# One core's attention and Mish MLP on Trainium2: the same steps in a newly annealed order

## The chip, the cores and the metric

The kernel runs on one core of a Trainium2 chip. Its five engines run side by side, each through its own instructions in order: TensorE (PE, matrix products), VectorE (DVE), ScalarE (ACT), GpSimd (POOL) and SyncE (SP, which only issues DMAs here). They meet at semaphores. The metric is the device time of one launch in microseconds, as the median of repeated runs.

## The reference, cut to what matters

```python
def _attn_ref(q, k, v):            # 8 batches, 8 heads, 576 rows, head size 64
    q_s = exp(q - max(q, axis=-1));  q_s /= sum(q_s, axis=-1) + 1e-09
    k_s = exp(k - max(k, axis=2));   k_s /= sum(k_s, axis=2) + 1e-09
    kv = einsum('bhsd,bhse->bhde', k_s, v)
    return einsum('bhsd,bhde->bhse', q_s, kv)

def _moe_ref(x, w_in, w_out):      # x 4608 x 512, w_in 512 x 2048, w_out 2048 x 512
    h = x @ w_in
    g = h * tanh(where(h > 20, h, log1p(exp(min(h, 20)))))
    return g @ w_out
```

The heads of the attention's result are laid side by side as the rows `x` of the MLP.

## The kernel before

The kernel is a set of small steps (functions such as `a_ktt`, `h_part`, `w_fetch`) and one long string, `ORDER` (line 23), of 2551 tokens. A loop at the end (line 971) takes the tokens one by one and calls the step that each names (dictionary `stages`, line 947) with its numbers; letters behind the numbers name the PSUM banks (a to h) that the step opens, or the engine (v, p, s) that it uses. Every step issues its instructions to its engines as it is called, and `manual_schedule` keeps that order. So `ORDER` is the order of every engine's queue, of the DMAs on SP's and POOL's queues too, and nothing else in the kernel decides when something runs, other than the waits that follow from data and buffers. Some tokens name the same step on another engine: `RL`, `RM` and `RS` make the low half of a weight on GpSimd, ScalarE or VectorE; `RO` and `RD` a weight's low part on GpSimd or VectorE; `GA` and `G` a copy on ScalarE or VectorE.

The products are made of high and low halves: each 32-bit factor is split into two parts in the multiplier's own format, and three of the four part products are summed in PSUM (the three matmuls of `h_part`, `out_part`, `first_product`, `second_product`). The weights come as 64-bit numbers and are put together in integer steps.

The stages, in the order in which PE goes through them:

- **The opening.** SP loads K transposed (`LK`), Q (`LQ`), V (`V`) and weights (`R`). K: `MK` (DVE, column maximum), `KA` (ACT, subtract), `KT` (PE, transposes), `EK` (ACT, exponential). Q: `MQ` (DVE), `SQ` (POOL), `EQ` (ACT), `Q` and `QZ` (DVE), `QM` (POOL), `T` (PE, transposes), `TC` (ACT, copy out of PSUM). Then `KP` (PE, K times V), `S` (DVE, scaled into `kvt`), `XP` and `XT` (PE, Q times it, the main rows and the tail rows), `Z` and `ZL` (ACT and DVE, the high and low part of `x`), `ZT` (ACT, the tail). A weight goes through `RA` (ACT), `RL`/`RM`/`RS`, `RB` and `RC` (DVE), `RH` (ACT, the high part), `RO`/`RD` (the low part). `FI` n (`idle`, line 403) runs n multiplications of 128 columns, two instructions each, whose result nobody reads. `EX` is one small exponential on ACT.
- **Three batches in the plain way.** `H` and `HM` (PE, `x` times `w_in`; token `H` 4f+t is the t-th quarter of the f-th column block), `Y` (ACT, Mish), `GA`/`G` and `GL` (high and low part), `O` and `OP` (PE, times `w_out`). Beside it the attention of the other batches goes on in pairs (`PX`, `PK` on PE; `QM`, `SQ` on POOL; `T` from 8 on by DVE), and the weights are mixed for the rest (`WW`, `WM`, `WH`, `WL`) and written to a DRAM buffer `ws` (`WK`, `WP`, DMAs on SP).
- **The other five batches, and the tail rows of all eight as a sixth, in three pairs (k = 0, 1, 2)**, by seven products of half-size blocks in place of eight. `A` k.n.p (PE, the first product, six matmuls) goes into the banks px, pz and py, and `C`, `J`, `N` take it out (ACT copy, DVE sum, ACT Mish). `GX`, `GH`, `GK` mix and split the result, `BB` k.f.p (PE, the second product) multiplies it with `w_out` blocks, `DP`, `DJ` and `DS` take the result out and store it. `BM`, `DK` and `DT` are the same for the last product, in halves. The weights for `A` and `BB` come back from `ws` through six slots: `F` e (`w_fetch`, line 813, a DMA of 512 KB on POOL's queue) may start when the last product that uses slot e - 6 is done, and the products of slot e wait for its landing.

Of the kernel before, what the change touches and what calls it, by code (L numbers as in the profile page):

```python
# [33 lines left out]
Y6 RC14 RL19 GA6 H28f GL5 R25 O4 RS18 RA16g GL6 RA15h RH14 RB16 RA18e RO14 RB15 RH17 RC16 RM30 H29 RC15 RO17 RM21 H30
RB18 RA19h R26 H31 R31 RH16 QM4 RB19 RM20 H32g RC19 Y7 H33 RO16 RM24 RC18 H34 RA21h G7 H35 RB21 O5 QZ5 Y8 RC21 RH15
QM5 GL7 RA20h G8 RA23e RO15 RH18 RB20 O6 RH19 RB23 RO18 WK1 GL8 RC23 RD19 RA24e RH21 H40g RB24 R27 WK0 H41 RC24 H42
RC20 RH24 H43 RH23 RO24 T4ef Y10 H36h TC4 LQ6 RO21 G10 R28 H37 RA22f RS22 L6 H38 RL31 GL10 V6 H39 RB22 O7 Y9 RC22 RL26
GA9 RH22 GL9 RM25 MQ6 RH20 T5ef MK6 RM27 RO20 H44h RA25g LQ7 MK7 TC5 ST2 H45 RB25 RO23 WK2 RA27e H46 RA26f RB27 O8 SQ6
# [5 lines left out]
OP13.0 ZT6 Z6 H60g MQ8 ST6 Z7 U8.0 OP14.3 WH1.1 MS8 H61 ZL6 H62 ZT7 MT8 WH1.0 ZL7 SQ8 H63 U8.1 OP14.2 WL1.0 EQ8 HM16h
Q8 LQ9 ST7 WL1.1 LK10 Y15 WP1.0 G15 WP1.1 HM17e GL15 Y16 RH31 V8 GA16 RO31 QW8 HM18f Y17 MK10 GL16 WM2.0p MQ9 OP15.1
Y18 QV8 OP14.0 MS9 WM2.1p OP15.2 OP15.0 WH2.0 KB10 QM8 OP15.3 EV0.0v EV0.1s WH2.1 HM19g G17 GA18 T8 KM10 WL2.0 MT9
GL17 WP2.0 SQ9 HM20h EV0.2v UE10.0 WK15 GL18 EV0.3s EQ9 PK6eb LQ10 OP16.0 S8 OP16.3 WL2.1 OP17.0 Q9 WP2.1 HM23f QW9
V10 MQ10 ES0.0 QV9 MS10 WW3v OP16.2 OP17.3 QM9 Y19 OP16.1 GA19 WM3.0p OP17.1 Y20 GL19 OP17.2 U10.0 WM3.1p HM21e T9
UE10.1 WH3.0 MT10 SQ10 GA20 OP18.3 WW4v EQ10 OP19.3 WH3.1 OP18.2 WL3.0 Q10 OP18.0 WP3.0 Y21 WL3.1 HM22g LQ11 GA21
U10.1 QW10 GL20 LK12 WP3.1 GL21 OP18.1 Y22 WM4.0p OP19.2 Y23 G22 PX8he QV10 GL22 QM10 OP19.0 Z8 OP20.2 Z9 ZL8 OP19.1  # L50
ZL9 OP20.1 G23 WM4.1p OP20.3 MQ11 PK8eh GL23 WH4.1 WW5v MS11 HM24g ZT8 MT11 WH4.0 T10 ST8 SQ11 S10 ES0.1 WL4.1 OP21.3
WL4.0 WP4.1 OP22.3 EQ11 ZT9 OP21.1 Q11 LQ12 WP4.0 OP23.3 QW11 HM25e WK13 QV11 MK12 QM11 KB12 WK14 OP20.0 KM12 T11
OP21.0 UE12.1 OP21.2 UE12.0 WM5.0p WK12 HM26h U12.0 WM5.1p MQ12 Y24 Y25 ST9 OP22.1 V12 Y26 OP23.1 WH5.1 MS12 WL5.1
# [983 lines left out]
```

## Time and profile before

| | us |
|---|---|
| median of three runs (791.91, 792.03, 793.3) | 792.03 |
| the profiled execution, its own time | 792.54 |
| its span, first to last instruction | 790.8 |
| chain that ended last: share of PE | 93% of the span |
| weight fetches `ws<-ws`, issue to landing (median of 172) | 4.5 |

A group's row in the profile gives the line, the engine, the operation, what it writes and reads, its shape, how many there are, the busy time and the mean of one. In a row of a timeline the first two numbers are the start and the length in microseconds, and the bracket at the end is the engine's idle time before it, with what ended it. Matmuls overlap: a stream of 512-column matmuls on PE starts one every 0.227 us (twelve in 2.72), though one alone is shown with some 0.39.

### The profile page before, as it was taken

What the parts mean: (1) busy time and instruction counts of PE and PEld (TensorE: products, weight loads), DVE (VectorE), ACT (ScalarE), POOL (GpSimd) and SP (SyncE); (2) the same over time, 40 slices, a digit from 0 to 9 for tenths busy, and PEclk for the clock granted to TensorE, in tenths of its full rate; (3) what the DMA queues carried; (4) which work ended last, traced back from release to release, by engine and by line L of the source; (5) the groups of instructions that cost most, each with busy time, mean ns of one, the idle gap of its engine ahead of it and who ended that gap; (6) DMA issues with size and microseconds to landing.
All of it is one profiled execution on the core that took longest, in us unless ns stands there. A gap on an engine that the chain in (4) does not pass through costs nothing.

```text
span 790.8 us, 12668 instructions
## 1 busy us (share of the span) xinstructions
PE 782.1 (99%) x4640; PEld 632.4 (80%) x4640; DVE 535.7 (68%) x874; ACT 496.5 (63%) x945; POOL 274.8 (35%) x350
## 2 busy tenths in 40 slices
...
GB/s 349 375 347 235 344 155 212 169 240 166 211 258 133 180 62 216 319 256 237 290 237 235 246 254 235 161 244 143 276 193 208 231 222 212 207 165 236 168 232 188
DMA packets 76685, 178.86 MB, mean 226 GB/s; under 512 B 15568, under 2 KB 28112, under 8 KB 76624
## 3 DMA queue, kind: packets, MB, share of 16 engines
q0 software_dynamic: 24768, 90.19, 36.3%
q1 hardware_dynamic: 51712, 87.74, 33.1%
...
q14 instruction: 25, 0.20, 0.1%
q10 hardware_dynamic: 144, 0.13, 0.0%
...
## 4 chain that ended last, share of the span: by engine, by line
PE 93%; DMA 2%; DVE 2%; ACT 1%; issue 1%; SPq 0%; POOL 0%; DVEq 0%; POOLq 0%; ACTq 0%
PE px L833 16%; PE ph L646 16%; PE po L684 15%; PE qx L850 12%; PE qz L850 8%; PE py L833 8%; PE qy L850 8%; PE pz L833 4%; PE px L533 2%; PE pt L568 2%; DMA ws<-ws 1%; DMA q<-in_q_dram 1%; PE pt L533 0%; PE pq L510 0%; DMA ws<-wi 0%
## 5 line engine op out<-in xcount | busy, mean ns | idle before, releaser
L816 POOL DMA_DIRECT2D ws<-ws x172 | 92.6, 540 | 337.1 <-PE qx L850 78.4
L833 PE MATMUL px<-xh,ws 128*128 128x512 f32 x384 | 129.0, 392 | 0.9 <-DMA ws<-ws 0.9
L883 ACT CAST gs<-g 128x1024 fp32r<-128x1024 f32 x84 | 87.2, 1052 | 66.2 <-PE qx L850 28.9
L219 DVE TENSOR_TENSOR gs<-g,gs 128x1024 fp32r<-128x1024 f32 x84 | 101.8, 1230 | 31.5 <-ACT gs L883 31.3
L684 PE MATMUL po<-wo,gh 128*128 128x512 f32 x384 | 119.9, 393 | 0.0
L850 PE MATMUL qx<-gs,ws 128*128 128x512 f32 x432 | 101.1, 389 | 0.0
L850 PEld LDWEIGHTS qx<-gs,ws 128*128 128x128 f32 x432 | 81.0, 188 | 17.6 <-issue 0.8
L646 PE MATMUL ph<-xs,wi 128*128 128x512 f32 x384 | 92.9, 392 | 1.1 <-DVE gl L219 0.7
L833 PEld LDWEIGHTS px<-xh,ws 128*128 128x128 f32 x384 | 72.1, 188 | 19.6 <-issue 2.5
L684 PEld LDWEIGHTS po<-wo,gh 128*128 128x128 f32 x384 | 71.1, 188 | 18.3 <-issue 3.2
L646 PEld LDWEIGHTS ph<-xs,wi 128*128 128x128 f32 x384 | 71.3, 188 | 17.7 <-DVE wc_in L271 1.3
L861 ACT COPY g<-px 128x512 f32<-128x512 f32 x72 | 41.1, 587 | 68.1 <-PE px L833 65.8
L865 DVE TENSOR_TENSOR g<-py,g 128x512 f32<-128x512 f32 x48 | 32.7, 684 | 63.7 <-PE py L833 38.8
L684 PE MATMUL po<-wo,gl 128*128 128x512 f32 x192 | 74.8, 390 | 0.0
L833 PE MATMUL px<-xl,ws 128*128 128x512 f32 x192 | 74.7, 389 | 0.0
L850 PE MATMUL qz<-gs,ws 128*128 128x512 f32 x288 | 67.7, 389 | 0.0
L850 PE MATMUL qy<-gs,ws 128*128 128x512 f32 x288 | 67.4, 389 | 0.0
L833 PE MATMUL py<-xh,ws 128*128 128x512 f32 x192 | 66.6, 390 | 0.0
L850 PEld LDWEIGHTS qy<-gs,ws 128*128 128x128 f32 x288 | 54.1, 188 | 11.2
L850 PEld LDWEIGHTS qz<-gs,ws 128*128 128x128 f32 x288 | 54.0, 188 | 11.2
L219 DVE TENSOR_TENSOR g<-g,g 128x1024 f32<-128x1024 f32 x48 | 57.7, 1217 | 1.9 <-ACT g L869 1.6
L491 POOL TENSOR_TENSOR qe<-qe,qs 128x576 f32<-128x576 f32 x24 | 29.6, 1231 | 74.2 <-DVE qs L487 45.3
(167 smaller groups left out, 1377.9 us busy)
## 6 DMA issues: line engine op xcount, KB each, us to landing
ws<-ws POOLq DMA_DIRECT2D x172, 512.0 KB, 4.5
...
```

What stands on the lines that cost most here:

```text
L219: eng.tensor_tensor(out, a, b, ALU.subtract)
L491: eng.tensor_tensor(q2, q2, z.unsqueeze(2).to_broadcast(list(q2.shape)), ALU.mult)
L533: nc.tensor.matmul((px, pt)[x][h][o], kvt[a, j], at[e + j]["qT"][x][a], start=True, stop=True)
L568: nc.tensor.matmul(pkv[i][j * D:(j + 1) * D], k, v_two[a, j, c], start=c == 0, stop=c == NR - 1)
L646: nc.tensor.matmul(gs[n], wi[f][:, a, t], x[:, z], start=t == 0 and i == 0, stop=t == HP - 1 and i == 2)
L684: nc.tensor.matmul(po[t], g[a][:, t * P:(t + 1) * P], wo[f][:, z], start=f == 0 and i == 0, stop=f == NF - 1 and i == 2)
L816: nc.gpsimd.dma_start(t.rearrange("p s z j c -> p s (z j c)"), ws[e % (NW // 2)].bitcast(F32R))
L833: nc.tensor.matmul(dst, w[:, a, j], xc[k, p][z][:, j].rearrange("p b s -> p (b s)"), start=p in (1, 2, 7) and j == 0 and i == 0, stop=j == ...
L850: nc.tensor.matmul(psb[key, k][m], w[:, a, m], g[:, z, f % 2], start=first and i == 0, stop=f == NH - 1 and i == 2, skip_group_check=p in ...
L861: nc.scalar.copy(g_quad(k, n)[q], psb[1, k, n])
L865: nc.vector.tensor_tensor(g, psb[2 if q == 0 else 7, k, n], g, ALU.add)
L883: nc.scalar.copy(t[:, 0], gq[k, h][G_PART[p]])
```

## The change

Only the string `ORDER` is replaced. The 2551 tokens are the same steps, but for 42 that do the same work on another engine, and the banks of some fifty are renamed; the counts of the `FI` tokens are 12, 3, 9, 4, 1, 1 before and 9, 1, 4, 12, 3, 1 after. 244 tokens keep their place; the others move 13 places on average, some writes of weights (`WK`) by up to 700. The last 70 tokens are the same. The new order is a new annealing run at a low temperature that starts from the order before, in a simulation whose DMA landings and instruction lengths are read from the trace of before. The parts at the opening, around `GL11`, around `F64` and around `F137`:

```diff
ORDER = """
-FI12a LK0 LQ0 LK1 LQ1 EX LQ2 LK2 LQ3 R0 LK3 MQ0 V0 V1 MK0 SQ0 MK1 R1 KA0 MQ1 KT0db EQ0 FI3a KA1 SQ1 Q0 EK0 KT1he V3
-MQ2 FI9a EK1 R2 QZ0 SQ2 MK2 EQ1 V2 Q1 KA2 QM0 EQ2 KT2hd R3 QZ1 RA0b MQ3 QM1 R4 T0ge EK2 Q2 FI4a RM0 R5 MK3 SQ3 TC0 R8
-KP0a QZ2 KA3 RB0 QM2 EQ3 T1fc R6 S0 KT3he TC1 Q3 RL1 R9 FI1d EK3 XP0gc RC0 RA1d QZ3 LK4 RH0 XT0ef RB1 QM3 T2ba Z0 R7
-KP2h RC1 ZT1 ZT0 Z1 RO0 ZL0 TC2 R10 FI1d ZL1 RM2 T3da PP S2 RA2b H0c RH1 RB2 H1 TC3 ST0 RO1 RS3 RA3g XP2ha RC2 RM4 R14
-RB3 RL5 H4b Z2 H5 Z3 R13 ZL2 RH2 XT2de ZL3 H2 RO2 ZT3 RC3 RA5h R11 H6 RA4f RB5 H7 ZT2 RL6 RH3 RB4 LQ4 RA6g H3 RC4 R15
-RA8d H8a RL8 RC5 H9 RD3 H10 RB6 Y0 RM7 H11 RB8 RL10 RH4 MK4 H12e RH5 RC6 H13 LK6 RA7f RO5 R12 RC8 Y1 H14 LK5 Y2 RB7
...
-RC25 RB26 WK5 RC26 RC27 H47 RD22 RH27 XT4ef RH26 H52g RO27 R29 ZT4 RH25 WK10 B6e H53 Y11 RL28 WW0v O9 MQ7 EQ6 WM0.0p
-WK9 KS6 ZT5 GA11 O10 WM0.1p WH0.0 Q6 RA29f WK7 RA28e QZ6 SQ7 WH0.1 RB28 RM29 RC28 EK6 H54 RO26 GL11 LK8 H55 RH28 RB29
-RO25 H48h WK11 EQ7 H49 Q7 RO28 H50 RC29 RW30 H51 RB30 H56e WL0.1 RH29 RC30 RW31 H57 WP0.1 WL0.0 H58 ST4 QZ7 H59 Y12
...
-XH1.4 A1.0.5 A1.1.2 N1.0.0 KB30 BB0.6.4 F66 C1.1.0 F63 C1.0.3 BB0.7.4 J1.0.3 QV28 A1.0.3 DJ0.2.0 QM28 DJ0.2.1 DS0.2.0
-A1.1.6 ST27 J1.1.0 F65 XL1.4 F64 A1.1.7 C1.1.2 T28 KM30 A1.2.2 F67 EQ29 A1.2.1 Q29 LQ30 A1.0.4 C1.2.0 F69 QW29 A1.1.5
...
-A2.3.4 F134 C2.5.0 A2.5.6 J2.3.2 F135 F138 J2.5.0 A2.7.1 GK2.1.1 N2.5.0 N2.4.2 N2.3.1 A2.5.7 A2.6.1 F137 A2.6.2 C2.6.0
-C2.5.2 A2.6.7 J2.6.0 F139 A2.5.5 A2.6.6 C2.5.3 J2.5.3 A2.5.3 C2.6.2 N2.5.3 N2.6.0 A2.6.5 F141 N2.4.3 F140 GH2.1.2
...
+FI9d LK0 FI1c FI4e LQ0 FI12d LQ1 LK1 LQ2 FI3c LK2 R0 MK0 LQ3 R1 MQ0 KA0 V1 KT0bh SQ0 EK0 LK3 MQ1 EQ0 SQ1 V2 MK1 V0 Q0
+KA1 R2 EQ1 MQ2 KT1af QZ0 EK1 SQ2 V3 MK2 RA0f Q1 R3 KA2 QM0 R6 RM0 QZ1 KT2dg MQ3 EQ2 QM1 R4 T0ch EX RB0 R5 TC0 MK3 SQ3
+T1ea EK2 Q2 TC1 KP0b RL1 QZ2 EQ3 LK4 RC0 R8 KA3 S0 RA1c QM2 KT3de RH0 Q3 XT0fh R7 EK3 XP0ag RB1 RO0 RM2 LQ4 QZ3 T2eb
+ZT1 RC1 Z0 KP2h QM3 ZT0 ZL0 RH1 R12 RA2f RO1 T3ad PP TC2 RB2 H0c R11 TC3 S2 H4b RM3 RC2 Z1 XP2ha R9 RA3e ZL1 RM4 RB3
+XT2df H1 R13 Z2 RL5 ZT3 FI1g LQ5 Z3 ZL2 H5 RH2 ZL3 H2 RA4g RO2 RC3 R10 H3 RB4 RH3 H6 RL8 RA5f RC4 H8a RB5 H9 MK4 RL6
+H10 Y0 RD3 LK6 RA6h H7 LK5 RC5 RA8g RL7 L4 H12e RB6 GA0 H13 RH5 R15 GL0 RA7f H11 RB8 RO5 R14 Y1 H14 RC6 ZT2 GA1 RB7
...
+R29 H52g WK1 RC27 RH26 H45 RD22 XT4ef WW0v H46 ZT4 ZT5 RM28 H53 WM0.0p RH27 MQ7 B6e H47 MK8 H48f RO26 Y11 H49 GA11 O9
+SQ7 GL11 KS6 EQ6 WM0.1p RA28h KB8 RB28 RO27 H50 EQ7 H51 WH0.0 RL30 KM8 Q7 O10 RH25 RC28 RA29e EK6 Q6 QZ6 RH28 H54 QZ7
...
+BB0.4.4 ZT26 XL1.5 BB0.5.4 J1.0.0 F61 F60 MT29 A1.0.6 F63 A1.1.1 C1.0.2 BB0.6.4 C1.1.0 ZT27 BB0.7.4 A1.1.6 DJ0.2.0 F65
+F64 QV28 A1.0.5 DJ0.2.1 A1.1.2 C1.0.3 J1.0.3 A1.0.3 J1.1.0 F66 QM28 A1.2.2 T28 N1.1.0 C1.1.2 XL1.4 A1.1.7 N1.0.1
+A1.1.5 F67 SQ29 A1.0.4 C1.1.3 A1.2.1 J1.0.2 EQ29 J1.1.3 LQ30 A1.1.3 Q29 C1.2.0 F69 V30 F68 J1.2.0 ST27 A1.3.1 DS0.1.1
...
+A2.6.1 C2.5.3 A2.5.7 A2.6.2 J2.5.3 F137 N2.5.3 A2.5.3 C2.6.0 F139 N2.0.2 J2.6.0 A2.6.6 N2.6.0 N2.4.1 A2.7.2 C2.6.2
```

More of the change, by code (lines that the diff above doesn't have):

```diff
@@ L34 @@
[L34 to L38, printed above, removed]
@@ L44 @@
[L44 to L48, printed above, removed]
@@ L49 @@
[L49 to L53, printed above, removed]
@@ new lines @@
+RA16g RL19 GA6 O4 RC17 RC14 RA15h RB16 RH17 R25 RH14 GL6 RO17 RC16 H28f RB15 RH16 RL20 H29 QZ4 RA18e H32g RC15 RS18
+H33 RA19h R26 RD14 RM21 H30 RB19 RO16 RH15 H31 RC19 H34 RL23 Y7 RB18 H35 GA7 RC18 RA21h O5 QZ5 RL24 Y8 RB21 RH18 GA8
+RC21 RO15 GL7 RA24h GL8 RA23e O6 QM4 RA20f RB24 RH19 RB20 RO18 RB23 MK6 H40g RO19 RC23 H41 RC24 R27 H42 RL22 RC20 RH24
+R28 H43 WK3 RS26 RH21 T4ef RD24 Y10 RL25 H36h MK7 TC4 H37 G10 RA22e LQ6 QM5 H38 GL10 ST0 H39 RB22 RA25g R30 O7 WK2 Y9
+RC22 RH20 GA9 RO20 RH23 GL9 RH22 RB25 RL27 RA26f T5he LK8 RD23 O8 TC5 LQ7 RB26 RA27e RO21 MQ6 RB27 SQ6 RC25 H44h RC26
@@ new lines @@
+MK14 OP24.3 Y26 OP23.2 WM5.1p G25 HM27f GL25 G26 WH5.1 GL26 WL5.1 OP24.0 WW6v Y27 OP24.1 GA27 OP25.0 GL27 PX10eg EQ12
+Q12 LQ13 PK10hf WP5.1 QW12 OP25.1 S12 V14 WH5.0 OP26.1 WK0 ZT10 Z10 WL5.0 OP24.2 KB14 QV12 OP25.3 KM14 MQ13 QM12
+UE14.0 OP26.3 ES0.2 Z11 HM28h WP5.0 U14.0 WM6.0p MS13 UE14.1 MT13 T12 ZT11 SQ13 OP25.2 EQ13 HM29f Q13 LQ14 WK14 QW13
+QV13 OP26.0 ZL10 QM13 OP27.0 U14.1 Y28 Y29 OP27.3 G28 WM6.1p LK16 WH6.0 OP27.1 GL28 HM30e ZL11 WH6.1 WL6.1 MQ14 WP6.1
+WL6.0 MS14 OP26.2 WP6.0 GA29 HM31h Y30 GL29 WK15 GA30 MT14 WW7v GL30 SQ14 OP27.2 WK13 Y31 MK16 OP28.0 WM7.0p GA31
@@ new lines @@
+WM9.0p PX14ed EQ16 WM9.1p WH9.0 LQ17 PK14fg XR14 KB18 HM36e WL9.0 V18 ZT14 XR15 KM18 Q16 WP9.0 UE18.0 GL35 WK9 QW16
+MQ17 ZT15 QV16 OP33.1 S16 OP32.2 OP32.3 Y36 Y37 OP33.3 WH9.1 OP33.2 WL9.1 OP34.2 WW10v WP9.1 OP35.2 UE18.1 OP34.1
+U18.0 GA36 WM10.0p HM39g MS17 U18.1 GL36 LK20 QM16 WH10.0 ST14 MT17 G37 SQ17 OP34.3 T16 OP35.3 WM10.1p EQ17 HM38e Q17
+LQ18 ST15 F0 WL10.0 QW17 GL37 WP10.0 WH10.1 QV17 OP35.1 MQ18 QM17 OP36.2 MS18 OP36.3 T17 HM40f WW11v Y38 WL10.1 GA38
+MK20 WP10.1 Y39 OP35.0 Y40 OP36.0 MT18 GL38 KB20 SQ18 OP36.1 G39 OP37.3 WM11.0p GL39 OP37.0 OP37.1 EQ18 WM11.1p OP38.3
@@ new lines @@
+GA40 LQ19 WH11.0 GL40 PX16eg WW12v PK16hf Q18 OP38.1 KM20 ZT16 WH11.1 MQ19 ST16 OP38.0 XR16 WL11.1 OP37.2 QW18 OP38.2
+UE20.1 QV18 OP39.2 XR17 QM18 OP39.3 UE20.0 HM41g MS19 ZT17 MT19 XH0.1 S18 WL11.0 T18 SQ19 HM42f WP11.0 ES1.1 EQ19 Q19
+LQ20 ST17 XL0.1 QW19 OP39.1 WP11.1 OP40.2 QV19 OP39.0 QM19 Y41 HM44e MQ20 U20.0 MS20 Y42 MT20 U20.1 GA41 T19 OP40.0
+LK22 WM12.0p WK10 HM43h GL41 G42 WM12.1p GL42 V20 SQ20 PX18gf Y43 Y44 MK22 OP40.1 OP41.2 G43 EQ20 OP41.0 WH12.1 LQ21
+GL43 OP40.3 KB22 ES1.2 Q20 OP41.1 WH12.0 OP41.3 QW20 OP42.0 XR19 QV20 OP42.2 XR18 KM22 WL12.1 OP42.1 GA44 MQ21 QM20
@@ new lines @@
+T23 A0.2.4 J0.3.0 WL14.1 WP14.1 A0.4.1 J0.2.2 N0.3.0 WL14.0 ES2.1 N0.0.2 A0.2.3 WP14.0 MS24 ST20 C0.4.0 MT24 PK22df
+SQ24 N0.2.1 F17 PX22ch F19 A0.4.6 EQ24 S24 XR23 LQ25 XR22 LK26 A0.4.7 C0.3.3 ST21 C0.4.2 J0.3.3 ES2.3 A0.5.2 ES2.0 F21
+Q24 WM15.0p QW24 A0.3.3 ZT22 ST22 WM15.1p A0.5.1 N0.1.0 N0.3.1 A0.3.4 C0.5.0 MK26 WH15.1 A0.5.6 J0.5.0 F23 F22 J0.3.2
+A0.4.5 QV24 C0.5.2 WL15.1 WH15.0 N0.2.0 MQ25 A0.4.2 N0.3.2 KB26 A0.5.7 J0.4.0 F20 MS25 F24 KM26 C0.4.3 QM24 A0.6.1
+N0.1.2 J0.4.3 F25 T24 A0.6.2 MT25 WL15.0 UE26.1 SQ25 A0.5.5 C0.6.0 UE26.0 F27 A0.4.3 C0.5.3 EQ25 J0.5.3 A0.6.6 LQ26
@@ new lines @@
+A1.1.5 F67 SQ29 A1.0.4 C1.1.3 A1.2.1 J1.0.2 EQ29 J1.1.3 LQ30 A1.1.3 Q29 C1.2.0 F69 V30 F68 J1.2.0 ST27 A1.3.1 DS0.1.1
+ST26 N1.0.0 N1.2.0 A1.2.7 GH1.1.0 C1.3.0 A1.2.6 A1.3.2 C1.2.2 F71 QW29 A1.2.5 A1.3.6 C1.2.3 F73 F70 J1.2.3 A1.2.3
+N1.2.3 C1.3.2 A1.1.4 N1.2.1 N1.1.1 A1.3.5 J1.1.2 F72 QV29 A1.3.7 MQ30 C1.3.3 N1.1.3 J1.3.0 A1.2.4 N1.3.0 F74 GH1.1.1
+A1.4.1 J1.2.2 F75 MS30 MT30 A1.3.3 QM29 A1.4.2 N1.3.1 C1.4.0 A1.4.7 J1.4.0 T29 N1.4.0 A1.4.6 N1.0.2 J1.3.3 F77 GK1.1.0
+A1.5.1 C1.4.2 F78 SQ30 A1.4.5 F76 PX28df EQ30 C1.5.0 LQ31 A1.3.4 C1.4.3 DS0.1.0 A1.5.6 J1.3.2 F79 KM30 J1.4.3 A1.5.2
@@ new lines @@
+GK1.7.3 BB1.5.7 GX1.2.2v F101 XL2.1 BB1.0.6 XR35 GH1.6.2 DJ1.0.1 GH1.6.1 BB1.6.7 GX1.3.2v DS1.0.1 DS1.0.0 BB1.7.7
+GK1.6.1 GK1.6.2 BB1.1.6 GH1.6.3 F103 F102 GX1.3.3v BB1.2.6 GH1.3.0 XH2.3 GK1.3.0 BB1.3.6 F104 GK1.6.3 BB1.4.6 GH1.5.0
+GK1.5.0 BB1.5.6 XA2.0v BB1.6.6 GX1.2.3v BB1.7.6 F106 XA2.1v BB1.0.3 DP1.2.0 XL2.3 DP1.2.1 GH1.5.1 BB1.1.3 F107 F105
+GH1.5.2 GK1.5.1 BB1.0.5 GH1.5.3 GX1.0.3v XH2.7 BB1.1.5 F108 GK1.5.3 BB1.2.5 GH1.3.1 GK1.5.2 BB1.3.5 GK1.3.1 F109
+XA2.2v BB1.4.5 GH1.3.2 GK1.3.2 BB1.5.5 GX1.1.3v BB1.6.5 GH1.3.3 XH2.5 GK1.3.3 BB1.7.5 XL2.5 BB1.2.3 GH1.4.0 DP1.1.0
```

187 lines of the change are left out of this document (84 added, 103 removed).

## The prediction

> **What bounds the kernel now.** I read the page first: the span and the engines' shares.
>
> ```profile
> span 790.8 us, 12668 instructions
> ...
> PE 782.1 (99%) x4640; PEld 632.4 (80%) x4640; DVE 535.7 (68%) x874; ACT 496.5 (63%) x945; POOL 274.8 (35%) x350
> ```
>
> TensorE (PE) is busy in 99% of the span, and every multiplication is there after the change too, so the order can only move what stands between them. Next I asked the waits of PE, to see how much that is.
>
> ```profile
> PE pk L436 <- ACT kt L430: 1.4, 2, 0.9
> PE idle L408 <- DVE kvt L208: 1.1, 1, 1.1
> PE px L833 <- DMA ws<-ws: 0.9, 1, 0.9
> PE ph L646 <- DVE gl L219: 0.7, 1, 0.7
> PE ph L646 <- DVE wc_in L271: 0.4, 1, 0.4
> ```
>
> Three of the five lie in the opening. In the whole stretch behind it PE is idle twice: 0.7 us and 0.9 us. That is nearly all a new order can win there. The end is fixed too: the last 70 tokens of both orders are the same. What is left is the opening, where a busy PE says little, since it also runs fillers (FI: multiplications nobody reads). So I took PE's timeline of the opening.
>
> ```profile
> 1.06 4.93 PE L408 MATMUL idle<-kvt 128*128 128x128 f32 x24 [1.06 <-DVE kvt L208]
> 6.88 0.72 PE L436 MATMUL pk<-ident,kt 128*128 128x128 f32 x4 [0.89 <-ACT kt L430]
> 7.54 0.83 PE L408 MATMUL idle<-ident 128*128 128x128 f32 x6
> 8.85 2.17 PE L408 MATMUL idle<-ident 128*128 128x128 f32 x18
> 26.04 11.18 PE L646 MATMUL ph<-xs,wi 128*128 128x512 f32 x48
> ```
>
> The first K transpose (KT0, line 436) runs at 6.88, and the dense stream begins at 26.04 with H2; H0, H1, H4 and H5 are done before. From there PE is full, so a microsecond lost ahead of 26.04 is lost at the end as well. Who sets 26.04? ScalarE (ACT): its timeline.
>
> ```profile
> 0.73 1.28 ACT L954 ACT_TABLE_LOAD   x1 [0.73 <-PEq L1022]
> ...
> 5.96 0.78 ACT L430 ACTIVATE kt<-kt,mxd 128x576 f32<-128x576 f32 x1 [3.73 <-DVE mxd L361]
> 6.70 0.74 ACT L465 ACTIVATE q<-q 128x640 f32<-128x640 f32 x1
> 8.01 0.58 ACT L442 ACTIVATE k<-pk 128x512 f32<-128x512 f32 x1
> 8.48 0.26 ACT L443 ACTIVATE k<-pkt 64x128 f32<-64x128 f32 x1
> 8.94 0.60 ACT L442 ACTIVATE k<-pk 128x512 f32<-128x512 f32 x1 [0.20 <-PE pk L436]
> 10.67 0.78 ACT L430 ACTIVATE kt<-kt,mxd 128x576 f32<-128x576 f32 x1 [0.32 <-DVE mxd L361]
> 16.04 0.58 ACT L524 COPY qT<-pq 128x512 f32<-128x512 f32 x1 [0.31 <-PE pq L510]
> 20.10 0.70 ACT L252 ACTIVATE raw_in<-raw_in 128x512 uint32<-128x512 uint32 x1
> 23.84 1.07 ACT L632 CAST xs<-px 128x512 fp32r<-128x512 f32 x2 [0.23 <-PE px L533]
> 24.80 0.63 ACT L284 CAST wi<-wc_in 128x512 fp32r<-128x512 f32 x1
> ```
>
> From KA0 (5.96) to the end of RH2 (25.43) are 19.47 us, with only 0.20 + 0.32 + 0.31 + 0.23 = 1.06 us idle: 18.4 us of work. ACT is the engine that paces the opening, and Z2 and Z3 (the 1.07 us at 23.84) are what H2 and H3 multiply.
>
> **Term 1, the opening: fillers ahead of KT0.** Both orders hold 30 fillers' counts, 60 multiplications. Before, FI12 (24 of them) stands ahead of KT0 and the others fill holes between transposes. After, 9 + 1 + 4 + 12 + 3 = 29, so 58, stand ahead of KT0 on PE's in-order queue. Their pace: the first 24 took 4.93 us. Later ones are faster: 18 took 2.17 and 6 took 0.83, so 12 took 1.34, 0.112 each. The other 34 then cost 3.8 us, and KT0 starts at about 1.06 + 4.93 + 3.8 less the overlap of neighbours (0.16) = 9.6 instead of 6.88: 2.7 us later.
>
> What queues behind: ACT's order after is KA0 EK0 EQ0 KA1 EQ1 EK1; before it was KA0 EQ0 KA1 EK0 EK1. EK0 reads KT0's result, so ACT, done with KA0, stands at EK0, and EQ0 and KA1, which it did at 6.70 and 7.34 before, stand behind it. EK0 follows a transpose's start by some 0.75 us: 10.4. From there ACT has to do up to RH2 what it did before, without KA0 (0.7) and with RM3 (0.7 by the row at 20.10; it replaces VectorE's RS3), ZT3 and EX (some 0.2 each): 18.8 us. RH2 then ends at 29.2 if ACT never waits, at 30.2 if it waits the same 1.06; it was 25.43. That is 3.8 to 4.7 later.
>
> I followed the other queues through the opening by hand with the rows' durations and found none to be the later one: V0, moved behind V2 on SP, is needed by KP0, and KP0 now waits for T1, which stands ahead of it on PE, until about 17.8; XP2 comes to about 26, Z2 to 28.2, the VectorE part ZL2 to 29.5, and H2 starts at about 29.3, with the same four H done. So the dense stream starts some 3.5 us later than 26.04. Lowest: KT0's 2.7 less all of ACT's 1.06 of idle time, 1.6. Highest: 4.7. I take +3.5, the one nearest to ACT's rows. EX, the first activation before, is moved behind EQ2; its table load (0.73 to 2.01) should now stand ahead of KA0, in idle time too, and both orders switch tables 44 times: 0, or 1.28 if the load comes behind KA0, before EK0, where KT0 still covers it.
>
> Can it be won back? ACT can; PE can't:
>
> ```profile
> 26.00:100.00 74.00, 73.30 (x408) 58.82 (x400) 66.17 (x113) 62.94 (x110) 59.58 (x46) 1.00 0.93 319
> ```
>
> Behind the opening ACT is busy 62.94 of 74 us and catches up, while PE is busy 73.30 and keeps its lateness.
>
> **Term 2, the two waits that go.** The chains of 76 to 96 and 476 to 498 us:
>
> ```profile
> 90.71 2.73 DMA ws<-wi
> 93.44 0.02 issue
> 93.46 0.69 DVE gl L219
> ...
> 486.95 1.08 POOL qe L491
> ...
> 488.64 6.17 DMA ws<-ws
> ```
>
> First: GL11 (line 219) stood on VectorE behind RB28, which waited, and H48 needs GL11's bank. After, H48 takes bank f instead, stands ahead of GL11, and bank f's last reader, RC26, has five H steps of PE work in hand; GL11 itself stands ahead of RB28. The keeping of weights that the chain runs through (WK9, WK10, WK0) is moved hundreds of tokens on, to 743 and later. Second: F65 and F64 stood on GpSimd behind QM28, which waited for VectorE; after, both are ahead of QM28. What is late next at these places has 0.5 us and more in hand by the order. So -0.7 - 0.9 = -1.6 (0 if others take their place).
>
> **Term 3, changes between small and large multiplications.** The same twelve H multiplications, without and with an attention piece ahead:
>
> ```profile
> 177.34 2.72 PE ph L646 x12
> 181.76 2.95 PE ph L646 x12
> ```
>
> 0.2 us for each such visit. Behind the opening there are 30 visits before and 27 after (PX and PK stand together more often): -0.6.
>
> **Term 4, new waits.** The weight ring has six slots; F may fetch when the slot's last user is done. By the order, the PE work between that and the first use was never under four blocks of six multiplications; after, it is three blocks at F137 (A2.5.7 to A2.7.2) and four at F20, F72, F119 and F140 (two such before).
>
> ```profile
> 469.11 1.36 PE py L833 x6
> DMA to landing us min/median/max: 3.4/4.5/7.7
> ```
>
> Three blocks are 4.08 us, four 5.44; a fetch takes 4.5 from issue to landing in the middle. F137 then stalls PE 0.4 us, more with the issue itself; the four others at landings beyond 5.4 only, perhaps one in four with 0.5 to 1: +0.9 in all (0, if all land in 3.4, to 2.5). Between 90 and 300 us of PE work there are 22 multiplications that open a bank or use an operand at most 0.7 us of PE work behind its last reader or writer in the order, against 10 before, of which none stalled: +0.4 (0 to 1).
>
> All other moved and exchanged steps (low parts between the three engines, G to GA and back, DMA order on SP) lie beside PE work with VectorE, ACT and GpSimd at 66, 63 and 60 of 74 us in the densest stretch; 0 each, and what they cost without that cover is inside term 4's ends.
>
> **Sum.** +3.5 - 1.6 - 0.6 + 0.9 + 0.4 = +2.6 us. The profiled execution took 792.54 us for a span of 790.8, so it would be 795.1, with a span of 793.4. The median of the runs is 792.03, half a microsecond lower; on it I forecast 794.6. With all lows -0.6 (791.4), with all highs +6.0 (798.0).
>
> **The rivals.**
> A, faster: landings, not ACT, set the opening. For it: V0 is later on SP, DMA is busy throughout. Against: ACT's 1.06 idle us in 19.47. Then KT0's lateness costs nothing, and -1.6 - 0.6 + 0.4 gives 790.2. It decides as soon as the dense stream starts less than 0.2 us later than 26.04; the win is whole if it starts no later.
> B, no change: the opening loses only the low end, 1.6, as ACT's idle time shrinks: 1.6 - 2.2 + 1.3 = +0.7, 792.7.
> C, the clock falls in the opening. With the fillers spent, PE stands idle between transposes: 10.3 to 12.6, 13.2 to 15.4 by my sums. The end of the span has a row of PE, and behind it two stretches without it:
>
> ```profile
> 779.74 6.96 PE L850 MATMUL qy<-gs,ws 128*128 128x512 f32 x30
> ```
>
> ```profile
> 788.00:790.00 2.00, 0.00 (x0) 0.00 (x0) 0.00 (x0) 0.00 (x0) 0.00 (x0) 1.00 0.39 131
> 790.00:791.00 1.00, 0.00 (x0) 0.00 (x0) 0.00 (x0) 0.00 (x0) 0.00 (x0) 0.66 0.00 0
> ```
>
> The last multiplication ends at 786.70, and the granted clock (third number from the end) falls behind 790, after more than 3.3 us of idleness; my longest hole is 2.3. If it fell, it would take a stretch like that of the first fillers (4 us) at half pace: 2 us more, 796.6. By the Trainium skill, TensorE: Matmul & The Clock Gate, section "HAM oscillation — how this bites in real kernels", idle gaps beyond about 3.4 us make PE run at half clock again; by that rule, with holes of 2.3, C doesn't come. The trace agrees as far as these two rows go.
> D, the old waits don't go but move, or new ones take their place: 1.6 to 2 more, 796.4.
>
> **How the numbers follow.** Forecast 0.50, A 0.16, B 0.18, C 0.05, D 0.11. A measurement of this kernel tells about 0.2% from no change, 1.6 us: faster is under 790.4, slower over 793.6. Faster: A nearly whole, 0.15. Same: B and the low part of the forecast, 0.25. Slower: 0.60. The range leaves out A's better half and the upper ends of C and D: 790.4 to 797.4.
>
> **What would show it.** Step 1: one row of fillers up to about 9.6, KT0 behind it, ACT idle before its line 442, the dense ph rows from about 29.5. Step 2: no wait of ph on gl near 94 and of px on ws near 494 (or 3 later). Step 4: a wait of pz on ws at A2.7.2, near 700. The forecast is wrong if KT0 starts by 7, or if the dense stream starts by 27.

## The result: 12.7 us slower, where 2.6 were forecast

| | before | after |
|---|---|---|
| median of the runs of this comparison (us) | 792.27 (4 runs) | 805.0 (803.75 to 806.41, 4 runs) |
| ratio after to before, 95% interval | | 1.0159 [1.014, 1.0179] |
| profiled execution, its own time (us) | 792.54 | 803.75 |
| its span (us) | 790.8 | 802.0 |

The forecast was 794.6 with a range of 790.4 to 797.4. The sign was right, the size wrong, and the time lies outside the range. The page of the changed kernel begins:

```profile
span 802.0 us, 12645 instructions
...
PE 784.2 (98%) x4640; PEld 633.5 (79%) x4640; DVE 537.9 (67%) x872; ACT 497.8 (62%) x946; POOL 280.7 (35%) x351
```

The work is the same; the engines are busy for about as long as before (PE 784.2 us, before 782.1). What has grown is what stands between PE's instructions. The waits of PE (what waited, for what, us in total, how often, the longest; the line numbers stand one lower than before, as the string is one line shorter):

```profile
PE pk L435 <- ACT kt L429: 4.7, 3, 2.0
PE qx L849 <- DMA ws<-ws: 1.8, 2, 1.1
PE pq L509 <- DVE gl L218: 1.7, 1, 1.7
PE px L832 <- ACT g L860: 1.2, 2, 0.8
PE py L832 <- DMA ws<-ws: 1.2, 1, 1.2
PE idle L407 <- DVE kvt L207: 1.1, 1, 1.1
PE px L832 <- DMA ws<-ws: 1.0, 2, 0.5
PE pq L509 <- POOL wo L218: 0.7, 1, 0.7
PE pz L832 <- DMA ws<-ws: 0.2, 1, 0.2
PE pqt L510 <- DVE wc_out L270: 0.2, 1, 0.2
```

Before there were five rows, of 4.5 us; these ten come to 13.8. The two old waits, `ph` on `gl` and `px` on `ws` near 494, are gone as foreseen, and the forecast's own new one is there: `pz` on `ws`, 0.2 us, is A2.7.2 waiting for F137. But three more rows wait for the weight ring, and four for VectorE, ScalarE and GpSimd.

To place all of it I counted **lost time**: at a moment t, t less the PE work done by then. The work is the sum over all matmuls begun before t, fillers left out, of the usual distance to the next one for that shape (the 33rd percentile of the kernel before). Waits, the slow restarts behind them and a halved clock all show in it.

| lost time (us) at | 30 | 120 | 500 | 780 |
|---|---|---|---|---|
| before | 18.2 | 24.6 | 48.0 | 51.3 |
| after | 22.3 | 30.7 | 53.4 | 62.7 |
| added in the stretch that ends there | +4.1 | +2.0 | -0.7 | +5.9 |

The differences are taken before rounding. The stretches add up to 11.3, and the span grew by 11.2. So a third came in the opening, half in the last stretch, where PE multiplies weights out of the ring.

**The opening.** PE's timeline of the changed kernel (start, length, what, count, and the idle time before it):

```profile
1.05 4.21 PE L407 MATMUL idle<-kvt 128*128 128x128 f32 x18 [1.05 <-DVE kvt L207]
5.06 5.01 PE L407 MATMUL idle<-ident 128*128 128x128 f32 x40
9.91 0.64 PE L435 MATMUL pk<-ident,kt 128*128 128x128 f32 x4
...
12.68 1.12 PE L435 MATMUL pk<-ident,kt 128*128 128x128 f32 x4 [2.02 <-ACT kt L429]
...
16.00 1.13 PE L435 MATMUL pk<-ident,kt 128*128 128x128 f32 x4 [1.99 <-ACT kt L429]
...
29.61 1.63 PE L645 MATMUL ph<-xs,wi 128*128 128x512 f32 x6
```

One block of fillers stands ahead of KT0, which starts at 9.91 (forecast: 9.6). The dense stream begins with H5 at 29.61. ScalarE meanwhile:

```profile
4.86 0.78 ACT L429 ACTIVATE kt<-kt,mxd 128x576 f32<-128x576 f32 x1
10.58 0.60 ACT L441 ACTIVATE k<-pk 128x512 f32<-128x512 f32 x1 [4.95 <-PE pk L435]
...
11.23 0.73 ACT L464 ACTIVATE q<-q 128x640 f32<-128x640 f32 x1
...
13.84 0.60 ACT L441 ACTIVATE k<-pk 128x512 f32<-128x512 f32 x1 [0.59 <-PE pk L435]
...
18.23 0.58 ACT L523 COPY kt_two<-pq 128x512 f32<-128x512 f32 x1 [0.99 <-PE pq L509]
```

It is done with KA0 at 5.64 and stands 4.95 us at EK0, with EQ0 and KA1 behind it, as the forecast had it. What I had not expected is the clock. Busy time of each engine by windows (after the fifth pair the granted clock of PE):

```profile
10.00:12.50 2.50, 0.66 (x6) 0.39 (x4) 0.51 (x1) 1.92 (x4) 0.00 (x0) 1.00 1.03 408
12.50:16.00 3.50, 1.34 (x5) 0.89 (x5) 3.40 (x11) 2.88 (x7) 2.38 (x2) 0.53 1.03 405
16.00:19.50 3.50, 3.50 (x17) 3.13 (x19) 3.20 (x8) 2.51 (x8) 3.41 (x4) 0.50 1.04 413
```

Half clock for some 7 us, and KT1 takes 1.12 us where KT0 took 0.64. The forecast gave that a chance of 0.05. ScalarE's two waits in this stretch, 0.59 and 0.99 us (rows above), are for transposes that PE runs at half clock.

**The ring.** The chain that ends with PE's wait at 570 us (start, length, what):

```profile
558.70 1.39 PE px L832 x6
560.09 2.73 PE qx L849 x12
562.82 0.39 issue
563.21 0.52 POOL ws L815
563.73 6.90 DMA ws<-ws
570.64 0.04 issue
570.68 1.43 PE qx L849 x5
```

The fetch that lands in 6.90 us is F88, for BB1.5.1. By its slot's last product it could have started at 556.0. But it is queued behind F90 on GpSimd, whose slot came free at 562.8 only, so it was issued 7.75 us after its own release. Five late fetches share this form: F68, F88, F97, F110 and F118 each stand last of two or three on GpSimd's in-order queue. From the trace, each token with its instructions (PE's delay is the time from the start of the multiplication before to the fetch's first one, less the usual 0.227 us; the waits in the views are some 0.16 shorter):

| fetch | issued after its slot's release | landing | landing before | PE's delay |
|---|---|---|---|---|
| F68 | 2.34 | 7.68 | 5.25 | 0.71 |
| F88 | 7.75 | 6.90 | 5.54 | 1.24 |
| F97 | 6.89 | 5.95 | 3.73 | 0.89 |
| F110 | 6.89 | 6.57 | 4.71 | 0.07 |
| F118 | 10.98 | 8.50 | 3.44 | 1.38 |

F119 (0.58) and F137 (0.35), issued at once, are the two that stood on the forecast's list.

### The profile page after: what moved, and what is told of

It reads as the page before. It is cut to its first block, busy times and chain, and to the rows that moved or that the text cites. A ratio compares the mean times of both kernels' runs of the same rounds, so it can differ in the third digit from the quotient of the medians.

```text
span 802.0 us, 12645 instructions
## 1 busy us (share of the span) xinstructions
PE 784.2 (98%) x4640; PEld 633.5 (79%) x4640; DVE 537.9 (67%) x872; ACT 497.8 (62%) x946; POOL 280.7 (35%) x351
## 4 chain that ended last, share of the span: by engine, by line
PE 74%; DMA 6%; ACT 4%; issue 3%; POOL 3%; DVE 1%; SPq 0%; DVEq 0%; POOLq 0%; ACTq 0%
PE po L683 12%; PE qx L849 12%; PE ph L645 12%; PE px L832 11%; PE qz L849 8%; PE qy L849 7%; PE py L832 5%; DMA ws<-ws 4%; PE pz L832 2%; PE pt L567 1%; PE px L532 1%; DMA xt_dram<-xt 1%; POOL ws L815 1%; ACT g L868 1%; DMA ws<-m_out 1%
## 5 line engine op out<-in xcount | busy, mean ns | idle before, releaser
L849 PEld LDWEIGHTS qz<-gs,ws 128*128 128x128 f32 x288 | 54.1, 188 | 11.2
L218 POOL TENSOR_TENSOR q<-q,qm 128x576 f32<-128x576 f32 (+1 forms) x32 | 41.8, 1306 | 55.0 <-DVE qm L377 27.2
```

The lines of the kernel that those rows point to most:

```text
L218: eng.tensor_tensor(out, a, b, ALU.subtract)
L849: nc.tensor.matmul(psb[key, k][m], w[:, a, m], g[:, z, f % 2], start=first and i == 0, stop=f == NH - 1 and i == 2, skip_group_check=p in ...
```

## The experiments

Each time is the median of its runs; "over before" is the difference to the kernel before on the same chip in the same comparison (its median lay between 792.35 and 793.06). The ratios carry intervals of some 0.0015 each way, 1.2 us, so differences of about 2 us between two changed kernels are near what can be told. The lost time is that of each kernel's profiled execution.

| kernel | time | over before | ratio, 95% interval | lost at 30 | 120 | 500 | 780 |
|---|---|---|---|---|---|---|---|
| 1 fillers spread | 805.01 | 12.0 | 1.0154 [1.0135, 1.0172] | 22.1 | 30.7 | 54.1 | 63.1 |
| 2 before, fillers in front | 795.34 | 2.3 | 1.0041 [1.0025, 1.0057] | 23.0 | 30.0 | 53.2 | 57.2 |
| 3 fetches at release | 803.7 | 10.6 | 1.0125 [1.0102, 1.0149] | 22.3 | 30.7 | 54.1 | 64.2 |
| 4 queues mended | 803.49 | 10.4 | 1.0129 [1.0108, 1.0149] | 22.5 | 30.7 | 53.4 | 62.7 |
| 5 early KT0, holes filled | 802.51 | 10.1 | 1.0131 [1.0112, 1.015] | 18.9 | 27.1 | 49.4 | 62.4 |
| 6 holes filled | 806.14 | 13.7 | 1.0173 [1.0158, 1.0188] | 21.8 | 30.3 | 54.3 | 63.3 |
| 7 old opening, new rest | 801.13 | 8.7 | 1.0122 [1.0089, 1.0155] | 18.0 | 27.1 | 50.0 | 59.5 |
| 8 new opening, old rest | 797.39 | 5.0 | 1.0067 [1.0052, 1.0082] | 21.6 | 28.7 | 52.8 | 56.3 |
| 9 half fetches | 796.49 | 4.1 | 1.0051 [1.0036, 1.0065] | 21.2 | 29.6 | 50.7 | 54.0 |
| 10 three repairs | 800.7 | 8.4 | 1.0108 [1.0091, 1.0124] | 18.7 | 27.5 | 50.7 | 59.7 |
| 11 before, two waits mended | 790.92 | -1.4 | 0.9982 [0.9973, 0.999] | 18.2 | 24.1 | 46.2 | 49.7 |
| 12 three products ahead | 797.88 | 4.9 | 1.0071 [1.0054, 1.0088] | 18.9 | 27.5 | 50.9 | 55.6 |

**1 and 2. Fillers, in the changed kernel and in the one before.**

```diff
-FI9d LK0 FI1c FI4e LQ0 FI12d LQ1 LK1 LQ2 FI3c LK2 ... KT0bh ... KT1af ... T0ch ... KT3de
+FI12d LK0 LQ0 LQ1 LK1 LQ2 LK2 ... KT0bh FI3c ... KT1af FI9c ... T0ch FI4e ... KT3de FI1c
```

> The changed order with its fillers put back between the transposes: FI12 ahead of KT0, FI3 behind KT0, FI9 behind KT1, FI4 behind T0, FI1 behind KT3; nothing else moved. Theory (the 58 fillers ahead of KT0 make the opening late, and the clock's fall is their consequence): KT0 at about 6 instead of 9.91, no half clock after 6 us, H5 and the dense stream at 26 instead of 29.6, and the time 3.5 to 4.3 us under 805.0: about 801. Rival (the new DMA order, V0 behind V2, or the new order of the ACT steps makes the opening late): H5 stays behind 28.5 and the time within 1 us of 805.

```diff
-FI12a LK0 LQ0 ... KT0db EQ0 FI3a ... FI9a ... FI4a ... FI1d
+FI9a FI1a FI4a FI12a FI3a LK0 LQ0 ... KT0db EQ0 ...
```

> The kernel before with 29 of its 30 filler counts put ahead of KT0, in the changed order's sequence; nothing else moved. Theory (the fillers): KT0 at 9.9, the dense stream 2 to 3.5 us later than 26.04, the time at 794.3 to 795.8 against 792.3. A clock that falls in a hole of 2 us between two transposes is to be seen here too if it is the fillers' doing. Rival (other parts of the opening): within 0.7 us of 792.3.

The first missed: KT0 came at 6.34, and yet H5 came at 29.37 and the time was 805.01. PE's timeline shows why it told nothing of the fillers. One that I had put behind KT3 needed a bank that VectorE still read, and the clock fell behind that hole (granted 0.50 from 20.8 to 24.2 us):

```profile
20.07 0.49 PE L407 MATMUL idle<-ident 128*128 128x128 f32 x2 [1.61 <-DVE wc_in L270]
```

It does show what a halved clock can cost: from the first row of XT0 to H0 PE took 5.24 us (20.49 to 25.73), and 3.68 in the changed kernel, where the clock was whole by then (22.29 to 25.97).

The second came as expected in its time, +2.3 us. Its profiled execution, 798.27, lies near the upper end of its seven (795.13 to 798.52), and KT0 came at 13.23 in it, not at 9.9:

```profile
5.41 7.98 PE L408 MATMUL idle<-ident 128*128 128x128 f32 x40
13.23 0.64 PE L436 MATMUL pk<-ident,kt 128*128 128x128 f32 x4
```

The 40 fillers took 7.98 us there and 5.01 in the changed kernel, so this trace is not that of the median. The clock fell in it too, as expected, behind a hole of 2.08 us ahead of KT2 (granted 0.51 from 17.5 to 21.0 us). So 17 filler counts moved ahead of KT0 cost time in the old order too.

**5 and 6. The late KT0 against the clock.** Both fill the holes ahead of KT1 and KT2, with banks that nobody reads then; kernel 5 also has an early KT0.

```diff
-MK0 LQ3 R1 MQ0 KA0 V1 KT0bh ... MQ2 KT1af ... QZ1 KT2dg
+MK0 LQ3 R1 MQ0 KA0 V1 KT0bh ... MQ2 FI14c KT1af ... QZ1 FI14e KT2dg
```

> The changed kernel with 12 fillers ahead of KT0 in place of 58, and with 14 fillers right ahead of KT1 and 14 right ahead of KT2, in banks c and e that no other engine reads then (no filler behind T0 or KT3, where the filler FI1c waited 1.61 us for VectorE in the kernel with spread fillers). So KT0 is early and both holes are filled. Theory that the late KT0 and the halved clock made the opening 4.1 us later: KT0 near 6.3, granted clock 1.00 to 30 us, first product H5 of the dense stream at 25.5 to 27 in place of 29.61, time 801 to 802. Rival, that what releases H5 is another chain (DMA or ScalarE's order of the annealed opening): H5 stays at 28.5 or later, time 804 or more.

> The changed kernel with all its fillers, and 14 more right ahead of KT1 and 14 right ahead of KT2, to fill the holes of 2.02 and 1.99 us. KT0 stays at 9.9. If the clock fell because of the holes, it stays at 1.00 from 10 to 20 us, and KT1 takes 0.7 in place of 1.12. Theory that the halved clock itself cost about 2 us: H5 at 27.5 to 28, time 802.5 to 803.5. Rival, that the late KT0 sets it alone through ScalarE: H5 within 0.6 of 29.61, time 804.4 to 805.

In kernel 6 the clock stays whole. The same three windows:

```profile
10.00:12.50 2.50, 2.50 (x25) 2.50 (x24) 1.26 (x2) 2.50 (x5) 0.00 (x0) 1.00 1.02 405
12.50:16.00 3.50, 3.50 (x33) 3.50 (x32) 2.98 (x10) 2.42 (x5) 3.14 (x3) 1.00 1.04 401
16.00:19.50 3.50, 3.50 (x60) 3.33 (x60) 3.01 (x7) 2.65 (x8) 3.38 (x3) 1.00 1.03 413
```

ScalarE's busy time (the fourth pair) is nearly that of the changed kernel, H5 starts at 29.18, 0.43 earlier, with KT0 itself at 9.15, and the time, 806.14, is no better than 805.0. That does not price the halved clock, though. Each row of 28 fillers takes 3.29 us, longer than the hole that it fills, so KT1 comes 3.71 us behind KT0 (2.77 in the changed kernel), and ScalarE waits for PE as before, 1.05 and 0.85 us. From KT0 to H5 kernel 6 takes 20.03 us, the changed kernel 19.70. What the traces do bound: in the changed kernel ScalarE waited 1.58 us for transposes at half clock, and from EK0 to KA3 it took 10.09 us, where kernel 1, whose clock was whole in that stretch, took 9.39. By these rows the halved clock cost an estimated 0.7 to 1.6 us; no run shows it alone. With KT0 early (kernel 5) the picture is another. PE's timeline:

```profile
6.02 0.64 PE L435 MATMUL pk<-ident,kt 128*128 128x128 f32 x4
...
22.40 1.63 PE L645 MATMUL ph<-xs,wi 128*128 128x512 f32 x6
...
26.04 6.18 PE L645 MATMUL ph<-xs,wi 128*128 128x512 f32 x26
```

The dense stream starts at 26.04 in place of 29.61, and the lost time at 30 us is 18.9 in place of 22.3. Kernels 5 and 6 differ only in the fillers ahead of KT0, and KT0 and H5 are both 3.1 us earlier in kernel 5. So the fillers ahead of KT0, through ScalarE, made the opening late; for the landings and the rest of its new order little is left (18.9 us lost at 30 us against 18.2 before, with KT0 at 6.02 against 6.88). Of the 3.4 us, 2.6 appear in the time over before (12.7 to 10.1), 802.5 where 801 to 802 was expected. In its profiled execution the ring took the gain back: 13.1 us lost from 500 to 780 in place of 9.2, with a wait of 2.3 us for F88 and half clock behind it.

**7 and 8. Opening and rest exchanged.** Tokens up to H5 from the one order, then all others in the order of the other.

```diff
 kernel 7: opening of before, up to H5
+          then all other tokens in the order of after
 kernel 8: opening of after, up to H5
+          then all other tokens in the order of before
```

> The opening of the kernel before (its tokens up to H5, with its fillers), followed by all other tokens in the changed kernel's order. By the count of time in which PE did no useful work, the changed kernel had lost 4.1 us more than the kernel before by 30 us, and 7.1 us more behind that. If the two parts add up: about 4 us faster than the changed kernel, 800 to 801 (7 to 8 over the kernel before), lag at 30 us 18.2. Rival, that the rest was planned for a later opening and only waits the more: 803 or more.

> The opening of the changed kernel (its tokens up to H5), followed by all other tokens in the order of the kernel before. If the two parts add up: the 4.1 us of the opening alone, 796.5 to 797.5. Rival, that the slack in the old order takes up a late opening (its later waits are on transfers): 794.5 or less; that the joint adds waits of its own: over 799.

Both theories of a sum hold, the first nearly: 8.7 for the rest alone (7 to 8 expected; its four runs lie between 799.98 and 804.86), 5.0 for the opening alone, together 13.7 where the change has 12.7. No later slack takes up a late opening, and the new rest loses whatever stands ahead of it.

**3. Every fetch at its slot's release.** Each `F` stands right behind the last product that uses its slot.

```diff
-... A1.1.7 N1.0.1 A1.1.5 F67 SQ29 ... C1.2.0 F69 V30 F68 J1.2.0 ...
+each F e (e over 5) directly behind the last product of slot e - 6
```

> The changed order with every weight fetch F put right behind the last product that uses its slot, so that GpSimd issues them in the order in which slots come free; nothing else moved. Theory (F68, F88, F97, F110 and F118 were late since they stand last in bursts on GpSimd's queue, long after their slots were free): these five waits of PE (0.7, 1.2, 0.9, 0.1 and 1.4 us) and part of F119's 0.6 go, the time is 4 to 5 us under 805.0: about 800.5. F137 keeps its wait of 0.35. Rival (fetches land late since the transfers of that stretch are slow whatever the queue's order): waits of the same sum at other fetches, within 1.5 us of 805.

All five fetches of the table are then issued 0.41 us after their release and land in 3.5 to 4.7 us, and their waits are gone. GpSimd's timeline, where the first row is F88, 7.4 us earlier than in the changed kernel:

```profile
556.29 0.59 POOL L815 DMA_DIRECT2D ws<-ws  x1 [3.42 <-PE px L832]
557.65 0.53 POOL L815 DMA_DIRECT2D ws<-ws  x1 [0.77 <-PE pz L832]
559.00 0.53 POOL L815 DMA_DIRECT2D ws<-ws  x1 [0.82 <-PE py L832]
```

But the time fell by about 2 us only, to 803.7, short of the 800.5 expected. The waits of PE name what took their place:

```profile
PE px L832 <- DMA ws<-ws: 2.7, 1, 2.7
...
PE qy L849 <- DMA ws<-ws: 0.8, 1, 0.8
```

The 2.7 us are A2.2.1 at 652, waiting for F119. Three slots come free within 2.7 us there, the third fetch lands in 7.73 us, and the order leaves some 5 us for it. This profile is of the slowest of the four runs (806.34, the others 801.52 to 804.46), and the clock is at half for 6.8 us behind that wait, so its lost time is above the median's.

**4. ScalarE's and VectorE's queues.** The steps that stood ahead of what T5, T7, A0.5.6 and A0.7.6 wait for.

```diff
-RA25g R30 O7 WK2 Y9 RC22 RH20 GA9
+Y9 GA9 RA25g R30 O7 WK2 RC22 RH20
-WL0.0 H59 WL0.1 ... WP0.1 ... WP0.0 Z5 RO30 ZL5 GL14
+H59 ... Z5 RO30 ZL5 GL14 WL0.0 WL0.1 WP0.1 WP0.0
```

(with it ZT22 and ST22 behind A0.5.6, and C0.7.0 behind N0.5.0)

> The changed order with four places of the ACT and DVE queues mended: Y9 and GA9 ahead of RA25; WL0.0, WL0.1 and their stores behind GL14; ZT22 and its store behind A0.5.6; C0.7.0 behind N0.5.0. Theory (each wait of PE is made by what stands ahead of the step it needs): the waits at T5 (0.8), T7 (1.8), A0.5.6 (1.0) and A0.7.6 (0.6) go, 3.5 to 4.2 us under 805.0: about 801. Rival (what is late there is the work itself, so the next step in the chain takes the wait): under half of it, 803.2 or more.

A miss: the rival's 803.2 or more came true. The profiled execution took 803.72, as the changed kernel's (803.75), and its lost time is the same at 120 and at 780. The wait at T7 fell from 1.7 to 0.5 us, and waits of 0.8 and 0.4 us came up right behind it:

```profile
PE pkv L567 <- issue: 0.8, 1, 0.8
...
PE pq L509 <- DVE gl L218: 0.5, 1, 0.5
```

What sets the stretch around T5 and T7 is not settled by this run.

**9. Half of each fetch.** The kernel leaves out half of the weights from F18 on.

```diff
-nc.gpsimd.dma_start(t.rearrange(...), ws[e % (NW // 2)].bitcast(F32R))
+n = 2 if e < 18 else 1
+nc.gpsimd.dma_start(t[:, 0:n].rearrange(...), ws[e % (NW // 2)][:, 0:n].bitcast(F32R))
-w = ring[t // 2][:, t % 2]
+w = ring[t // 2][:, t % 2 if t < 36 else 0]
```

> The changed kernel, with only the first half of each weight fetch from F18 on brought in, and used twice (the second product of a pair multiplies the first one's weights, so half of the weights are left out; each instruction of PE keeps its shape, and each fetch its place). Theory that PE's lost time behind 480 us comes from fetches that are issued late behind others and then land in 6 to 8.5 us: landing falls to 3 to 4, the five waits on ws vanish, and the 5.9 us by which the changed kernel loses more than the kernel before between 500 and 780 us go: 798.5 to 800.5. Rival, that the issue alone is late or that PE waits there for banks and splits: 802 or more.

The fetches' landings (all 172, with the 18 whole ones) and PE's waits, which no longer name `ws`:

```profile
DMA to landing us min/median/max: 2.8/3.3/6.9
```

```profile
PE pk L435 <- ACT kt L429: 5.0, 3, 2.1
PE pq L509 <- DVE gl L218: 2.3, 2, 1.7
...
PE px L833 <- ACT g L861: 0.5, 1, 0.5
```

From 500 to 780 us it loses 3.3 us, as the kernel before does (3.3), where the changed kernel loses 9.2. All 5.9 go, with every fetch issued as late as in the changed kernel. So that stretch is the ring (smaller fetches also leave other transfers more room, which this run does not separate); the time fell by 8.5 as the profile's opening and middle were also 2.7 better.

**10 and 12. The three repairs together, and the order of PE's own products.**

> The changed kernel with all three repairs: 12 fillers ahead of KT0 and 14 ahead of each of KT1 and KT2; every fetch from F6 on right behind the last user of its slot; and the order of ScalarE's and VectorE's queues mended at T5, T7, A0.5.6 and A0.7.6. Alone they gave 2.5, 1.3 and 1.5 us. If they add: 799 to 800.5. Rival, that what one gains is lost again at the next late landing: 801.5 or more. That the changed order is better than the old one once its waits are mended: below 793.

```diff
-... C2.0.3 N2.1.0 J2.0.3 GH2.1.0 A2.2.1 XL2.4 A2.2.2 F125 C2.2.0 C2.1.2 A2.0.4 A2.1.5 A2.0.3 F124
+... C2.0.3 N2.1.0 J2.0.3 GH2.1.0 A2.0.4 A2.1.5 A2.0.3 F124 A2.2.1 A2.2.2 F125 C2.2.0 C2.1.2
```

(XL2.4 moves behind J2.1.0)

> The kernel with all three repairs, and A2.0.4, A2.1.5 and A2.0.3, whose weights have long landed, ahead of A2.2.1 (XL2.4 with them). There PE stood 3.04 us at 649.04 for F119, which was issued at once when its slot came free, as the third of three slots within 2.7 us, and landed in 7.1 us; the order leaves 5.0 us between the last use of that slot and A2.2.1. Theory that this part of the loss is the order of PE's own products, which no place in GpSimd's queue can mend: the wait goes with its halved clock behind it, 3.0 and 1.7 us: 796 to 797. Rival, that the later A2.2.1 and its slot only hand the wait on: 799.5 or more.

The three repairs gave 4.3 us together, a little less than their sum (2.5 + 1.3 + 1.5 by their times; 800.7, where 799 to 800.5 was expected). The F119 wait stayed, 2.7 us, and the clock was at half behind it:

```profile
652.90:656.30 3.40, 3.40 (x10) 2.63 (x9) 0.00 (x0) 1.07 (x2) 0.00 (x0) 0.50 0.30 111
```

Three products put ahead of A2.2.1 took both away, for another 3.5 us over before (8.4 to 4.9), nearer the theory than the rival though 1 us short of it. What is left of the ring in its waits:

```profile
PE qy L849 <- DMA ws<-ws: 0.7, 1, 0.7
...
PE px L832 <- DMA ws<-ws: 0.4, 1, 0.4
```

It is still slower than the kernel before (1.0054 at the least). By the lost time of its profile, 0.7 of the 4.3 us that are left stand in the opening, 2.2 between 30 and 120 us and 1.4 behind 500 us, and nothing in the new order makes up for them.

**11. The kernel before with its two waits mended.**

```diff
-WH0.1 RB28 RM29 RC28 EK6 H54 RO26 GL11 LK8
+WH0.1 GL11 RB28 RM29 RC28 EK6 H54 RO26 LK8
-DJ0.2.0 QM28 DJ0.2.1 DS0.2.0 A1.1.6 ST27 J1.1.0 F65 XL1.4 F64 A1.1.7
+DJ0.2.0 F65 F64 QM28 DJ0.2.1 DS0.2.0 A1.1.6 ST27 J1.1.0 XL1.4 A1.1.7
```

> The kernel before with its only two waits behind the opening mended: GL11 ahead of RB28 on VectorE, and F65 and F64 ahead of QM28 on GpSimd. PE's 0.86 us at 93.1 and 1.06 us at 493.7 go: 790.3 to 791 with the kernel before at 792.4. Rival, that the next slowest fetch or the later RB28 takes their place: within 0.5 us of the kernel before.

790.92 (11 runs, 790.69 to 791.62) against 792.35: 1.4 us faster, which beats both kernels. Behind the opening PE's waits are down to three of 0.2 us:

```profile
PE px L533 <- DVE gl L219: 0.2, 1, 0.2
PE pkv L568 <- DVE xs_odd L635: 0.2, 1, 0.2
PE px L833 <- ACT g L861: 0.2, 1, 0.2
```

## Where the prediction was right and where it failed

- **Term 1, the opening, +3.5 (1.6 to 4.7): right in mechanism and place, low in size.** KT0 came at 9.91 (9.6), H5 at 29.61. The loss was 4.1 by lost time and 5.0 by kernel 8 alone (its interval 4.1 to 6.5). Kernel 5 shows that the early KT0 brings it back. The size was 0.6 to 1.5 too low: behind EK0 the term allowed ScalarE 0 to 1.06 us of idleness, and it stood 1.58, for transposes at half clock.
- **Term 2, the two waits that go, -1.6: right.** Both are gone, and kernel 11, which mends only these two in the old order, gains 1.4.
- **Term 3, fewer visits, -0.6:** not measured by itself. From 120 to 500 us the change loses 0.7 less than before, with one delay of 1.06 us mended and two new ones there (0.98 and 0.59 us, for ScalarE; the first behind a landing of `xt_dram<-xt` of 7.71 us). That leaves room for a gain of this size.
- **Term 4, new waits, +0.9 for the ring and +0.4 for banks, is the step that failed.** The ring cost 5.9 (kernel 9; the seven delays above make 5.2 of it). "By the order, the PE work between that and the first use" was the only thing I counted, from a slot's release to its first use, with a list of the fetches under 5.5 us. That list was right for what it held: F137 cost 0.35 (0.4 in the forecast), F119 0.58. But the five others have 10 to 20 us from release to use. They were late since the order puts them behind others in GpSimd's queue, 2.3 to 11 us after their release, and since they then land in 6.0 to 8.5 us. I counted the slot's clock and not the queue's, though I had used the queue in term 2 for F64 behind QM28. Kernel 3 shows the place in the queue to be the cause for these five, and kernels 10 and 12 show the second half: once they are mended, F119's short lead at three releases in a row costs 2.7 us of waiting and a halved clock behind it, which is what term 4 did look at and put at "perhaps one in four with 0.5 to 1".
- **"All other moved and exchanged steps ... 0 each" failed too, by 2.0 us at 30 to 120 us, and by more if the wait of 0.7 us that went there is counted.** T5 and T7 wait 0.7 and 1.7 us (the rows of `pq` that name GpSimd and VectorE); of these 90 us VectorE is busy 82.3, and was 78.0 before. Kernel 7 has these waits with the old opening as well, so they come from the order behind it. Kernel 4 shortened the second to 0.5 us, others took its place and the lost time stayed; which step sets them stays open.
- **Rival C, the fall of the clock, 0.05 and 2 us:** the fall came, and its price is not settled. I refused it because my longest hole was 2.3 us and the end of the span showed a fall only behind 3.3 us of idleness. Kernel 6 does not price it, as its fillers outlast the holes; ScalarE's rows give an estimate of 0.7 to 1.6 us, which lies inside the 4.1 of the opening. The page of the Trainium skill that I cited, TensorE: Matmul & The Clock Gate, section "HAM oscillation — how this bites in real kernels", asks for no idle gap beyond about 3.4 us; by it the clock should have held. This trace disagrees: two holes of 2.02 and 1.99 us, with PE busy 0.66 of the 2.50 us around the first, were enough.
- **Rivals A and B did not come; D, new waits for 2 us more, came in kind, at several times that.** The range missed since its upper end was made of term 4's own upper end (2.5), which came from the same list. "With all highs +6.0" also kept term 2 at -1.6; with that term's own high of 0 it is +7.6, 799.6, and still too low.

The landings explain how such an order could look good where it was made. From issue to first use it leaves the five fetches 5.2 to 7.3 us (use less issue, less PE's delay). With the landings that the same fetches had in the trace of before (last but one column of the table) each would have been in time, by 0.2 to 3.8 us. That is an argument from the two traces; no run held the landings fixed. The other traces bear it out: between the changed kernel and kernels 1, 4, 5, 6 and 7, which keep its order of fetches, the landings of the same fetch correlate with 0.87 to 0.95, and between the kernel before and kernels 2, 8 and 11 with 0.83 to 0.90. Between the changed kernel and the one before it is 0.16, and 0.30 between the changed kernel and kernel 3. So a landing repeats as long as the order does, and changes with it.
